# A spectral and attention kernel on one core: the inverse feature transform split into two lanes of 64 contraction rows, and a new instruction order

## The chip, the cores and the metric

One core of a Trainium2 chip runs the whole program. The metric is the device time of one execution in microseconds (us); smaller is better. Shown for the kernel before are three runs and one profiled execution.

## What is computed

The input x has 2048 rows of 640 features. Two results are mixed by a gate: a dilated local attention (32 heads of 20, each row looks at 8 rows two apart), and a spectral filter: a two-dimensional real Fourier transform of x, a multiplication by a table of complex weights, and the inverse transform.

```python
g = sigmoid((x * gate_w).sum(-1, keepdims=True))
q, k, v = split(x @ wqkv)
a = softmax(q k / sqrt(20), over 8 rows 2 apart) v @ wo
b = irfft2(rfft2(x) * (w_r + 1j * w_i))
return g * a + (1 - g) * b
```

## The kernel before, in words

The 2048 rows are handled as 16 row blocks j of 128 rows (row 16p + j of the input stands on partition p). The work falls into stages whose instructions are interleaved:

- **qkv**: x times wqkv in float32r, 8 units of 8 row blocks, 15 matmuls of 480 columns each, stored to DRAM (tile qkvd).
- **fold** and **cols**: the features are folded into their cosine and sine parts, and a 128-row transform along the rows is made; the result stands in SBUF as zg, 5 tiles t of 128 feature rows for each j.
- **attend** (16 calls, half for even j, half for odd j): VectorE (DVE) and GpSimd (POOL) make the products and sums of the attention, two row blocks at a time; results go to DRAM (tile od).
- **freq** (line 637, 16 blocks g): matmuls v and u (feature transform), sums ab on DVE, matmuls x and z (the second part of the row transform), the product with the weights, partly on POOL (tile P) and partly on DVE (in place in z), then two DVE instructions that write the tile s as P plus z and P minus z (lines 714 to 719), and five matmuls g that take 128 columns of s each as stationary operand and whose result ScalarE (ACT) copies back into zg.
- **spatial** (line 761, 16 row blocks, odd j first): the inverse feature transform and the last part of the inverse row transform. The feature part is six matmuls into two PSUM tiles, oa and ob (o1 and o2 in the code), from the stationary zg[:, t, j] and the table gt. The 640 feature rows are a cosine-even part (161), a cosine-odd part (160), a sine-even part (159) and a sine-odd part (160) one after another, so that the tiles t = 1, 2 and 3 of 128 rows straddle two parts. A straddling tile makes a 322-column matmul or two of 161. ACT copies oa and ob to the tile os, four matmuls of 161 columns make ha and hb, and DVE, ACT and POOL finish the even blocks. Banks 0, 1 and 2 of PSUM serve oa and ob in turn.
- **project_even, project_odd** (lines 843 and 857): the attention result of one row block is loaded (tile ot), transposed on TensorE (PE) into oT, multiplied by wo (30 matmuls of 320 columns in float32r, woa and wob), and added to the spectral part. An odd block can only be projected when all of its attention has been stored, and the odd blocks come last.

Matmuls of float32 operands (u, v, x, z, g, oa, ob, ha, hb) stand in the trace as two records each, one after the other: two passes, each with its own weight load (LDWEIGHTS, on the row PEld). float32r matmuls are one record.

The order in which all of this is issued is not the order of the code. Every instruction is recorded with its engine (class Plan, line 164), and ORDER (line 204), a compressed table of numbers found beforehand, says in which order they are issued. Each engine then runs its own instructions in that order. Nearly all rows of the trace carry the line of the recording helper (L385), so they are told apart by tile names.

Of the kernel before, what the change touches and what calls it, by code (L numbers as in the profile page):

```python
# [31 lines left out]
def dft_tables():  # L32
# [98 lines left out]
    gt = np.zeros((640, 644))
    gt[0:161, 0:161] = np.cos(tau * np.outer(ke, d) / D) * ck(ke)
    gt[161:321, 161:322] = np.cos(tau * np.outer(ko, d) / D) * ck(ko) * (d < 160)
    gt[321:480, 322:483] = -np.sin(tau * np.outer(kb, d) / D) * ck(kb) * ((d > 0) & (d < 160))
    gt[480:640, 483:644] = -np.sin(tau * np.outer(ko, d) / D) * ck(ko) * (d > 0)
    gt = np.concatenate(
        [gt[0:128, 0:161], gt[128:256, 0:322], gt[256:384, 161:483], gt[384:512, 322:644], gt[512:640, 483:644]], 1
    )
# [70 lines left out]
HQ(%xOkCb5Ti|9M&74oX@)~%FC+g&Um>cIj7Th&a$THElCM_Qxh94S8@_R$YuH^AlZ29A62|gtX_GwKt861v*&%|Lj%A~%)Ju4ard*J9-%@(h(=zcz=9{hy8`{2ylZ=~+70?!1ipBf(&
zwb}8-f;L(FVHcuzwYP7?2%s*U{nv&ECs$KBfw^t@z;C&Xf&zSgn_WXO0Ra-A{p=`KSTo&WCxLcHX{frWWSucqtk!hm#2nHJeX5P<a5rX;@Kti_Yl8ko7HnBP?BD0BCR!|nSp+9pO(On  # L210
7C*Q$o$wOs&SmSBdiC|DHG?D8$uS*E_ccd=5LY{i^BiXwbd{r0)D57<l%^E2DaY|53+8~ZxRJddAoRNdJYPz%5Lvh5W}S={Qu`$OJ}cwneg)RxR)(xpZMXtIs%DRMvJ7u?%%!@^1B8h@
(qlVz@tLYv`rnaOHo>WRfe{k*SBQiEnDF!z+o6MsFAJ=(MehAC+OQk;gfj{$D4Y9E8C&GfcpM}t1W|C%hJ#;L!7aan3ZqicP~xB7_Qnrj(tTe<@R?W&V{($jS4EF-5t#TOP0?OuT|3Qa
eIT(hT>jCQrecqER6AALUaUC?)=4v!RW)w9%$6TmkX}rmdZ1<A!<Ce0_LGFT-55A$ndz>!p$dHdxh1>o=3<(6z*KuxX86ZbhMDSB?~D@~6mK>u#>!XP<ORCokbE-Ovd^FevYd6|yTLNh
6LqbJKy?z;o)=#fxd)}q(t!E7s4(3|QOszQKMHHgt&?pyfYSMq-!@LPp=HMQOrhAsZ-JWy-C3Mc^Z`{5!$bngKocKj*>1lOfpe>gL<4DAk0)0!w_E-I8Ix5zA0pAPHAB79wZiA}lY^=h
Std;TST@mvK(Izv+y2xl{ZkLjAJfK%G&=WMvx-dxg6DMA424jO9cS?4TWJptst&`UzGq$ZfJ_rYlV4K31$NLXrgHytE*H`DST?S8Z+_yEBRpdjK2A~uXM4Nj32C4N!P4z2;Hqn$;QEkU
x#r;cod7g-0_+HHSjTx0G?wMOQFZ}koI>bLqzm3R1#oY}9`o)-A1NE;d6CRy2FU=-R;2owOP)Xp5@L{{lo`pBpk%V|R6g=MDVwD`bNH=OjT}S9%<^i$H2}^WSgi-blEMMxNCWOt@KVe#
HqSpv<!^C>%lNmv7RSF7$EOxNC{yKe#`U(Lx+?J!T>!ZP9DRYha-KfY6f?D)z+1)BTY#H0H8P_on~L7A?2-f-TVGlJ$NYiPg`Ivs?eZmoz*1s%9Xd;!3V#C-+$0Brl2%!N#H_A1i{L@S
P#-7P*l5}1Q+W5C%(=qlbU3pZ%otQHBXliSa7Eq92vyz1<`-h2wlnrTN(?T$K{1wyGNT3yESJ?d;(Zw=a_uas{jBg++Q~Nj2jh-_=z=SgoGX(xs<sgT2K8=TN&l`u^j-}yWbYSO(5cEw
hVcGl#lx!tpndKnI3W6}4nYMD+Pk`P27A{L32W`ao5f1Lx*Nb1X()n(JDUZ2O2az;7O<uub@cq%>A*E(_tL!Qq_R=1wNX@G<vau7PJDCp_$;h81hHJ;PIGy_$BYC9!FRj&Q%d@dloNT&
V}(@XS$iJK7_UBeT9exaHe0ZCd>(H!PSGFR8O~kQ=y2V-@rw&$Jg2mnKHs;xrCurTIvRujMxI%zzSsUAbNQyk@KBwL05WxN*Sm)5I2Xq^XZjzH)Ihl#)t51ss6A^!b?3)adQa(X1?V`Q  # L220
wEf(@vgv8sXd>1A(Inx$aDsF9o|pp|HZf+o&w(aEY-(nPPdJX2mvN>(E_fL#$UQPvI|Oa9cnbzr-e$^;-WQD_g83Pq)JF@6puq4=iw_oAzI4h0IpY+hbO=V@zz#KK7T>Y)df*No_7zw#
J`ZNS1m5yd>sTzrvwN&$9|njAQz>w>cl%q7wQZn?8p!=9m>5`9rRfIf_1}m*K9QWX2p$bk-U|1B1Z(^)NFjGTUi*=`v=?z{hl`I|qiO|ofbK~N2V}%VS*t!h=6?gk(z$O~7sEFHmYj%6
MNgL}676SI+-J!42{U}iie@2JyD7wX?tWyweu6+;9xiJSQlECBlw3cU6JNL9Qbq$0tUe_bx^QVlnRQ^tl#ei^!;Uy@((9<|ywE43$z4IgNR)3HBAWp^wA5G)i`pF3l<h}x3OgiJc*rTp
yDIhR4d;b1#P9;B=Fn!{JagvZWQ8Dna+>C8?PWN5+e!O%eKQFD7&UwCI9EJuzf24eM=px5vm)*=iSJQOsoOrV0(&B;X_MREg42C+90%XRnO_)k_RRKzcw`jk&FlJtxyJ@dT+yf~v((s8
-2h}>WX&Km>`JDrIZsB~HyMCyj)w7Emh<Bxtc+@vJ<-~GPXyd<K2@BwUFJSEEbOSLf-}5Tj30C4oH>gKhj@`yM0lgO1I|~8Uz5d)n(Ap~u7*R$VC*4V^uL@BrFYVSXJ!#;GPx$-`iB^*
2MiYfr5xOz@(Hn_ZO=uraJXL7TjCH2Oo22&4b<5GbESU)fMy@w<%JD=kBRvs^7YntD5lPeG0~#A(Y7f~=u1vSN3y;*%B)if3ZHyCNgsIjl_GRnl%27NSP+9t2PA;2H4bS5GyaV=>j*#x
*M~~EY1!7%?esLp+*GX}o-QD6C&^J6=;H8X|6(A(`yZi}Z}faaS0?Gjqv@lj&ep&tv$=yAF_CROwlnc;Gg~`p{^9llwa}e7zb`&fYr`LIz+M4&!D;pBW0~8c-9pQAVK~5|Lst>X_XHJf
BbHYtz@n{+NemE;D#YqvNyi@TUL%=x!c}A)W#~0YXI_9y%G_JmIy7up9F-wz0Ko(;nI?_m?Kd3a(}245c2v@Jf1OP32?$)b@4&S%LtI4Xl7SDnL8i5%lEDj)>G1TqOFDWr8uzjy&O3Nm
d$+wYoEer$Aq-KST1DqGF`N6nbu3i9J1y!73cVHXcW7RCc*0zmf=AnkP~}&rJ5)<G5jD!ivtsQGa!*YrUZ<x(O%YP2uxAQgki#<4cU6)m;~U+_$c%HUxDD2C>6*du+*nLhT21G%FSMTx
F9o90(I?=4__Uh>X7zl2S;|3%g?xk&&ZNy<yz%i{Sl87#;Hq(*dX#-S;0K7k`-=_DNmtn_cWizA<)OfVpjTP3DV~JDA&$35ndX-;RJ~3efGwiJ5Ht%!mBpiuzqzwAm%V<N$YT+%N<y?-  # L230
L$<-n`T;@{9ha=_DU5Caogirb*l5ll(=hVGvPaUVHGn@TTk@(O%Cg>+!F&Z>^a}MWs*HoAIXZ*IGmD&KQ1$s5UlW<f%b`0L6Zo}XxY*ejMiL6wZB3VWksk25LDcc$*m+|kO*MiA5qM!R
E4&I$iUB%e=t-&vI#oE3omS`8qhKNa{&xtjquCoj@gt~4hPP`#R?lah{_Fr2NG)2)6j`)6xWw-bn!#53kreFmg|f%8{Hi9hP;wz{AL5rvcI#V0DymT1c(Kucy<*0`8=s--Bri8zDH~#v
%-FB#M0Qq%ICg_IFP2C48|n56Sm9Um9k2fiPvpqah%)KEUW1~=uV*6=QB*z{Al8lvW9Q;ye=6Tp=v>L79H5IQ5X|z~#8hpnJr+Ga_QrkC4`Rhv7#WXovCK>ybSs8B6l~NOoIP)O5Fr!S
+}fcYgLx<p#v>wbK=gW?vhdCXZVtgKhsHNHj%~Qolp5+lQ(hjj51#p5_1_2~j|^=(cHJD!9j9&qpZdcxvk%!cXv8;;W{9m%oyJFbB38c|mac656_T8#{}Kg@00
# [732 lines left out]
```

## Time and profile before

| | |
|---|---|
| three runs | 453.57, 454.58, 453.53 us; median 453.57 |
| profiled execution, span | 454.1 us, 0.1% above the median |
| PE busy | 441.2 us, 97% (weight loads PEld 391.8 us) |
| DVE, POOL, ACT busy | 409.8 us, 363.9 us, 211.9 us |
| instructions | 7249, of them 2440 matmul records |
| DMA | 110.75 MB in 73956 packets |

A matmul's record lasts from its start to its modelled end, and records of neighbouring matmuls overlap; how long one really holds PE is the distance from its start to the next one's start. Idle time of PE is what the view of waits lists.

### The profile page before, as it was taken

Reading aid. Unit: us, or ns where it says so; the run is one execution under the profiler, and the core shown is the slowest. Engines: PE = TensorE matmul, PEld = TensorE weight load, DVE = VectorE, ACT = ScalarE, POOL = GpSimd, SP = SyncE. Lnnn points to the kernel's source line nnn. Section 1 sums busy time; section 2 is a strip of 40 time slices with the busy share of each in tenths; the row PEclk is TensorE's granted clock in tenths of the full one; section 3 lists DMA queues with packets and bytes.
Section 4 is the critical chain, followed back from the end, with each engine's and each line's share of the span. In section 5 each row is a group of like instructions: output and inputs, shape, how many; then the busy total and the mean of one; then the engine's idle time right before and its main releaser. Section 6 shows DMA issues by size and latency. Waiting matters only on the chain. (4 is left out here: it accounts for less than half of the span.)

```text
span 454.1 us, 7249 instructions
## 1 busy us (share of the span) xinstructions
PE 441.2 (97%) x2440; PEld 391.8 (86%) x2440; DVE 409.8 (90%) x519; ACT 211.9 (47%) x561; POOL 363.9 (80%) x316
## 2 busy tenths in 40 slices
PE   9999999999999999999998989999989999999996
PEld 6888888888889888899886769998877899999996
DVE  4899999899999999999978989999999997899484
ACT  4723165625226463255356666667554655342110
POOL 1158895899899898988977898976899998889810
PEclk9999999999999999999998999999999999999999
DMA  8998999887968979679979778989883331365932
GB/s 312 401 383 268 340 330 377 305 264 237 272 183 272 340 217 316 181 216 320 303 220 294 240 230 250 297 245 320 258 257 105 85 97 54 118 207 134 296 123 87
DMA packets 73956, 110.75 MB, mean 244 GB/s; under 512 B 21296, under 2 KB 50992, under 8 KB 73920
## 3 DMA queue, kind: packets, MB, share of 16 engines
q1 hardware_dynamic: 40192, 69.32, 46.8%
q10 hardware_dynamic: 32816, 36.97, 26.1%
q0 software_dynamic: 912, 4.00, 2.4%
q8 instruction: 19, 0.31, 0.3%
q14 instruction: 17, 0.14, 0.1%
HBM read 72.51 MB, written 32.84 MB: 232 GB/s over the span
## 5 line engine op out<-in xcount | busy, mean ns | idle before, releaser
L385 PE MATMUL qkv<-w,xo 128*128 128x480 f32 (+1 forms) x480 | 110.6, 385 | 0.0
L385 PE MATMUL qkv<-w,xe 128*128 128x480 f32 (+1 forms) x474 | 104.3, 382 | 0.0
L385 PEld LDWEIGHTS qkv<-w,xe 128*128 128x128 f32 x474 | 89.3, 189 | 15.2 <-ACT xe L385 0.9
L385 PEld LDWEIGHTS qkv<-w,xo 128*128 128x128 f32 x480 | 89.7, 189 | 13.8 <-ACT zg L385 0.2
L385 ACT COPY ev<-qkv 128x480 f32<-128x480 f32 x64 | 34.9, 558 | 48.3 <-PE qkv L385 35.9
L385 PE MATMUL woa<-wo,oT 128*128 128x320 f32 x240 | 47.2, 318 | 0.4 <-ACT oT L385 0.4
L385 PE MATMUL wob<-wo,oT 128*128 128x320 f32 x240 | 46.9, 315 | 0.2 <-ACT ya L385 0.2
L385 POOL TENSOR_TENSOR P<-P,wp 128x963 f32<-128x963 f32 (+1 forms) x16 | 35.4, 2212 | 6.6 <-DMA P<-X 4.0
L385 PEld LDWEIGHTS woa<-wo,oT 128*128 128x128 f32 x240 | 37.7, 188 | 1.1 <-ACT oT L385 0.6
L385 PEld LDWEIGHTS wob<-wo,oT 128*128 128x128 f32 x240 | 37.8, 188 | 0.6 <-ACT ya L385 0.4
L385 POOL TENSOR_TENSOR fx<-fx 128x160 f32<-128x160 f32 (+1 forms) x16 | 12.8, 818 | 24.2 <-DMA fc<-in_t_fc 17.1
L385 POOL TENSOR_TENSOR w<-raw,w 128x480 fp32r<-128x480 f32 (+1 forms) x20 | 24.8, 1262 | 5.3 <-ACT w L385 5.3
L385 ACT CAST oT<-oTp 128x384 fp32r<-128x384 f32 (+1 forms) x32 | 13.4, 427 | 30.9 <-PE oTp L385 17.3
L385 PEld LDWEIGHTS g<-mm,s 128*128 128x128 f32 x150 | 21.0, 190 | 7.1 <-ACT zg L385 5.0
L385 PE MATMUL g<-mm,s 128*128 128x128 f32 x150 | 23.5, 280 | 3.1 <-ACT zg L385 3.0
L385 DVE TENSOR_TENSOR oT<-oTp,oT 128x384 fp32r<-128x384 f32 (+1 forms) x32 | 15.2, 485 | 11.0 <-ACT oT L385 10.7
L385 PE MATMUL oa<-gt,zg 128*128 128x161 f32 (+1 forms) x96 | 24.0, 344 | 0.0
L385 PE MATMUL ob<-gt,zg 128*128 128x161 f32 (+1 forms) x96 | 22.0, 344 | 0.0
L385 PE MATMUL u<-bt,zc 128*128 128x240 f32 (+2 forms) x96 | 21.1, 335 | 0.7 <-DVE ab L385 0.7
L385 PE MATMUL v<-bt,zc 128*128 128x240 f32 (+2 forms) x96 | 21.5, 335 | 0.2
L385 DVE TENSOR_TENSOR fx<-fx 128x642 f32<-128x642 f32 (+2 forms) x24 | 19.2, 798 | 0.7
L385 PEld LDWEIGHTS u<-bt,zc 128*128 128x128 f32 x96 | 16.9, 199 | 2.9 <-PE g L385 0.9
(304 smaller groups left out, 1107.6 us busy)
## 6 DMA issues: line engine op xcount, KB each, us to landing
qkvd<-ev ACTq DMA_DIRECT2D x32, 480.0 KB, 4.8
wp<-in_ws SPq DMA_DIRECT2D x16, 642.0 KB, 5.9
raw<-in_wqkv SPq DMA_DIRECT2D x25, 240.0 KB, 5.9
fx<-in_x SPq DMA_DIRECT2D x8, 641.0 KB, 7.9
ot<-od SPq DMA_DIRECT2D x16, 320.0 KB, 3.9
P<-X ACTq DMA_DIRECT2D x30, 160.5 KB, 4.6
fd<-fx POOLq DMA_DIRECT2D x6, 640.0 KB, 5.6
f<-fd SPq DMA_DIRECT2D x6, 640.0 KB, 6.1
```

The costliest lines, as they stand in the source:

```text
L385: p.dve.memset(w, 0.0)
```

## The change

The feature rows are laid out anew. Lane 0 (partitions 0 to 63 of each tile t) holds 160 cosine rows and then 160 sine rows of the even frequencies, lane 1 (partitions 64 to 127) the same of the odd ones; 320 rows are exactly five strips of 64. The middle strip (t = 2) is half cosine and half sine and needs 322 columns, the other four need 161. The table `gt` becomes 128 rows of 966 columns. In `spatial` each row block now makes ten matmuls with 64 contraction rows each, five with partitions 0 to 63 into oa and five with partitions 64 to 127 into ob.

In `freq` the tile s has to be written in that layout: four DVE instructions of 256, 64, 64 and 256 elements take the place of two of 321 and 319, and one ACT instruction writes a single column. Block g = 0 has a few more. The copies of oa and ob into os become contiguous, os rotates over five buffers (before, three), and the whole of ORDER is new.

```diff
+STRIPS = (2, 0, 322), (0, 0, 161), (1, 0, 161), (3, 161, 161), (4, 161, 161)
...
 ORDER = """
-T>t<81poj4|NsC0{{R31`zHT%QmDPk&^9H>y=H*?`Lk%9Gnl%)B_CdQV7rLsIrdLM6sJFoVB8Rk|2U=URH5DLwHy3}>N|I2375U5sNENOZ_r>p;QjNS0Qt^d&3_BFn1BL!{U(U9<aW#`
...
+{Wp48S^xk5{}S0j0stWa8~^|S5YJf5;2m=ecU=Gg0s6R6M52`fc4RAY6qg`NyHIB4o@A#NU6@5pcjA0+(rn3g<Hq*N?);S;<qAiG*|7vsBv}=d&%uk^>u_xVVkn+f*DZ$G;1pjN+A)sRJO)fP3tQBb
...
-        self.osr, self.hor, self.hyr, self.yer = n("raw", 3), n("x", 4), ring("x4", "x5"), ring("x6")
+        self.osr, self.hor, self.hyr, self.yer = ring("raw0", "raw1", "raw2", "ev0", "ev1"), n("x", 4), ring("x4", "x5"), ring("x6")
...
-        V.tensor_add(s[:, 0:321], P[:, 0], z)
-        V.tensor_sub(s[:, d0 : d0 + 319], P[:, 0, 2:], z[:, 2:])
+        V.tensor_add(plus, strips(P[:, 0], 0), strips(z, 0))
...
+            V.tensor_sub(mixed[:, :, 32:64], parity(P[:, 0], 0, 32), parity(z, 0, 32))
+        V.tensor_add(mixed[:, :, 0:32], parity(P[:, 0], 128, 32), parity(z, 128, 32))
+        V.tensor_sub(minus, strips(P[:, 0], 32), strips(z, 32))
+        A.activation(out=s[:, 288:289], in_=z[:, 0:1], func=AF.Identity, bias=P[:, 0, 0:1])
...
-        mm(o1[:, 0:322], 1, gt[:, 161:483], True, False)
-        mm(o1[:, 0:161], 0, gt[:, 0:161], False, False)
-        mm(o1[:, 161:322], 2, gt[:, 483:644], False, True)
-        mm(o2[:, 0:322], 3, gt[:, 805:1127], True, False)
-        mm(o2[:, 0:161], 2, gt[:, 644:805], False, False)
-        mm(o2[:, 161:322], 4, gt[:, 1127:1288], False, True)
+        c = 0
+        for t, a, n in STRIPS:
+            for o, k in ((o1, slice(0, 64)), (o2, slice(64, 128))):
+                T.matmul(
+                    o[:, a : a + n], zg[k, t, j], gt[k, c : c + n], start=(t == 2), stop=(t == 4), skip_group_check=True
+                )
+            c += n
```

How the order changes is shown at two places. The first is PE at the start of the spatial stage. oa1 and ob1 are the two PSUM tiles of row block 1, oa3 and ob3 those of block 3, ha1 and hb1 what follows from os1; one row is one matmul of the program, "x2" two of them. Before:

```order
L385 MATMUL g15_3_815<-mm13_771,s15_813 128x128 x2
L385 MATMUL oa1_872<-gt_327,zg_211 128x322
L385 MATMUL oa1_872<-gt_327,zg_211 128x161 x2
L385 MATMUL oa3_878<-gt_327,zg_211 128x322
L385 MATMUL ob1_873<-gt_327,zg_211 128x322
L385 MATMUL ob1_873<-gt_327,zg_211 128x161 x2
L385 MATMUL oa3_878<-gt_327,zg_211 128x161 x2
L385 MATMUL ha1_875<-os1_874,fct_71 128x161
L385 MATMUL ob3_879<-gt_327,zg_211 128x322
L385 MATMUL ha1_875<-os1_874,fct_71 128x161
L385 MATMUL hb1_876<-os1_874,fct_71 128x161
L385 MATMUL oa5_883<-gt_327,zg_211 128x322
```

and after the change:

```order
L384 MATMUL g15_3_815<-mm13_771,s15_813 128x128 x2
L384 MATMUL oa1_872<-gt_327,zg_211 128x322
L384 MATMUL ob1_873<-gt_327,zg_211 128x322
L384 MATMUL oa1_872<-gt_327,zg_211 128x161 x2
L384 MATMUL ob1_873<-gt_327,zg_211 128x161
L384 MATMUL oa3_878<-gt_327,zg_211 128x322
L384 MATMUL ob1_873<-gt_327,zg_211 128x161
L384 MATMUL oa1_872<-gt_327,zg_211 128x161
L384 MATMUL ob1_873<-gt_327,zg_211 128x161
L384 MATMUL oa1_872<-gt_327,zg_211 128x161
L384 MATMUL ob1_873<-gt_327,zg_211 128x161
L384 MATMUL oa3_878<-gt_327,zg_211 128x161 x3
```

The matmuls of oa and ob, which stood between those of ha, hb, wo and the transposes, now stand in nine runs over all row blocks, alternating between the lanes for the most part; the first seven runs hold 18 to 30 of the 160 matmuls each, the last two 4 and 6.

The second place is DVE in the frequency stage at block 1. ab0 are the sums of the block three steps later, pr and o tiles belong to the attention. Before:

```order
L385 RECIPROCAL g_73<-g_73 128x16
L385 TENSOR_TENSOR z1_609<-z1_609,P1_607 128x321
L385 TENSOR_TENSOR s1_617<-P1_607,z1_609 128x321
L385 TENSOR_TENSOR s1_617<-P1_607,z1_609 128x319
L385 TENSOR_TENSOR ab0_641<-u0_640,vs0_639 128x321 x2
```

and after the change:

```order
L384 TENSOR_TENSOR z1_609<-z1_609,P1_607 128x321
L384 TENSOR_TENSOR ab0_641<-u0_640,vs0_639 128x321
L384 TENSOR_TENSOR s1_617<-P1_607,z1_609 128x2x32
L384 TENSOR_TENSOR s1_617<-P1_607,z1_609 128x2x2x64 x2
L384 TENSOR_TENSOR s1_617<-P1_607,z1_609 128x2x32
L384 TENSOR_TENSOR ab0_641<-u0_640,vs0_639 128x321
```

The two instructions that write s1 have become four, and the first of the two that write ab0 has moved ahead of them.

## Rows read from the trace of the kernel before

**Rows 1.** Page, part 1: busy time, share of the span, instructions of each engine

```profile
span 454.1 us, 7249 instructions
...
PE 441.2 (97%) x2440; PEld 391.8 (86%) x2440; DVE 409.8 (90%) x519; ACT 211.9 (47%) x561; POOL 363.9 (80%) x316
```

**Rows 2.** What PE waited for, whole span: engine, releaser, us, times, longest

```profile
PE g L385 <- ACT zg L385: 3.0, 5, 1.0
PE x L385 <- DVE ab L385: 2.0, 1, 2.0
PE z L385 <- DVE t L385: 1.2, 1, 1.2
PE warmed L385 <- DVE warm L385: 1.1, 1, 1.1
```

**Rows 3.** Busy us by stretch: length, PE, PEld, DVE, ACT, POOL, clock, DMA, GB/s

```profile
220.00:260.00 40.00, 37.12 (x180) 31.27 (x179) 35.48 (x44) 22.60 (x69) 32.19 (x29) 0.96 0.86 265
260.00:346.00 86.00, 81.87 (x522) 73.66 (x521) 80.64 (x128) 53.15 (x147) 75.73 (x56) 1.00 0.84 258
346.00:409.00 63.00, 62.43 (x391) 56.90 (x390) 56.68 (x77) 30.36 (x79) 56.11 (x46) 1.00 0.34 105
```

**Rows 4.** The chain that ended last, from 346 us on: start, us, what

```profile
371.64 0.55 PE ha L385 x4
...
448.29 1.92 PE wob L385 x13
450.23 0.55 DVE y L385
```

**Rows 5.** PE in order of time, 364 to 368 us: start, us, what

```profile
365.80 0.70 PE L385 MATMUL oa<-gt,zg 128*128 128x322 f32 x2
366.34 0.44 PE L385 MATMUL ha<-os,fct 128*128 128x161 f32 x2
366.61 0.44 PE L385 MATMUL oa<-gt,zg 128*128 128x161 f32 x2
```

**Rows 6.** Group on PE by shape: count, busy, mean ns of one record

```profile
L385 PE MATMUL oa<-gt,zg 128*128 128x161 f32 x64 | 13.5, 299 | 0.0
```

**Rows 7.** Weight loads (PEld) and PE around 362 and 411 us, in order of time

```profile
361.85 0.33 PEld L385 LDWEIGHTS ha<-os,fct 128*128 128x128 f32 x2
...
361.71 0.44 PE L385 MATMUL oa<-gt,zg 128*128 128x161 f32 x2
...
410.91 0.19 PEld L385 LDWEIGHTS woa<-wo,oT 128*128 128x128 f32 x1 [0.59 <-ACT oT L385]
410.91 0.42 PE L385 MATMUL woa<-wo,oT 128*128 128x320 f32 x1 [0.35 <-ACT oT L385]
411.01 0.19 PEld L385 LDWEIGHTS wob<-wo,oT 128*128 128x128 f32 x1
...
411.17 0.31 PE L385 MATMUL wob<-wo,oT 128*128 128x320 f32 x1
```

**Rows 8.** Groups on DVE and ACT by shape: count, busy, mean ns

```profile
L385 DVE TENSOR_TENSOR s<-P,z 128x321 f32<-128x321 f32 x15 | 7.3, 486 | 0.9 <-POOL P L385 0.2
L385 DVE TENSOR_TENSOR s<-P,z 128x319 f32<-128x319 f32 x15 | 7.2, 480 | 0.0
...
L385 DVE TENSOR_TENSOR ye<-ho 128x160 f32<-128x160 f32 x8 | 2.3, 317 | 0.0
...
L385 ACT COPY z<-qkv 128x1 f32<-128x1 f32 x16 | 2.5, 162 | 1.7 <-ACT ev L385 1.7
```

**Rows 9.** SP's queue, stores and loads of the attention result, in order of time

```profile
421.66 0.37 SPq L385 DMA_DIRECT2D od<-o4b  x1
...
427.00 0.32 SPq L385 DMA_DIRECT2D ot<-od  x1
...
431.51 0.33 SPq L385 DMA_DIRECT2D ot<-od  x1
```

More of the change, by code (lines that the diff above doesn't have):

```diff
@@ L129, in ck @@
         return (np.where((k == 0) | (k == 320), 1.0, 2.0) / (S * D))[:, None]
[L131 to L138, printed above, removed]
+    lanes = np.zeros((2, 320, 322))
+    for lane, k, fits in ((0, PERM[1:161], (d > 0) & (d < 160)), (1, ko, d > 0)):
+        c = np.cos(tau * np.outer(k, d) / D) * ck(k) * ((d < 160) | (lane == 0))
+        s = -np.sin(tau * np.outer(k, d) / D) * ck(k) * fits
+        lanes[lane, 0:160, 0:161], lanes[lane, 160:320, 161:322] = c, s
+    lanes[0, 160] = np.repeat([1.0, 0.0], 161) / (S * D)
+    lanes = lanes.reshape(2, 5, 64, 322)
+    gt = np.concatenate([lanes[:, t, :, a : a + n].reshape(128, n) for t, a, n in STRIPS], 1)
     f = np.float32
@@ L209 @@
[L209 to L216, printed above, removed]
@@ L354, in work @@
         S.dma_start(self.sign, ins["t_sign"])
-        self.bt, self.gt = self.one("bt", 1288, tag="e0"), self.one("gt", 1288, tag="e1")
-        S.dma_start(self.bt[:, 0:1122], ins["t_bt"])
+        self.bt, self.gt = self.one("bt", 1122, tag="e0"), self.one("gt", 966, tag="e1")
+        S.dma_start(self.bt, ins["t_bt"])
         S.dma_start(self.gt, ins["t_gt"])
@@ L714, in freq, with parity, strips @@
         s = self.s12r.next(f"s{g}", 768)
-        d0 = 321
-        if g == 0:
-            d0 = 449
-            G.memset(s[:, 384:449], 0.0)
-        V.tensor_add(s[:, 0:321], P[:, 0], z)
-        V.tensor_sub(s[:, d0 : d0 + 319], P[:, 0, 2:], z[:, 2:])
+        def parity(a, k, n):
+            return a[:, 1:321].rearrange("p (b k) -> p b k", b=2)[:, :, k : k + n]
+        def strips(a, k):
+            return parity(a, k, 128).rearrange("p b (t r) -> p b t r", t=2)
+        plus, mixed, minus = (s[:, 128 * t : 128 * t + 128 * n] for t, n in ((0, 2), (2, 1), (3, 2)))
+        plus, minus = (q.rearrange("p (t b r) -> p b t r", t=2, b=2) for q in (plus, minus))
+        mixed = mixed.rearrange("p (b r) -> p b r", b=2)
+        V.tensor_add(plus, strips(P[:, 0], 0), strips(z, 0))
+        if g == 0:
+            other = s[:, 640:768].rearrange("p (b r) -> p b r", b=2)
+            G.memset(s[:, 256:384], 0.0)
+            G.memset(s[:, 640:768], 0.0)
+            for b in range(2):
+                V.tensor_sub(other[:, b, 33 - b : 64], parity(P[:, 0], 1 - b, 31 + b)[:, b], parity(z, 1 - b, 31 + b)[:, b])
+        else:
+            V.tensor_sub(mixed[:, :, 32:64], parity(P[:, 0], 0, 32), parity(z, 0, 32))
+        V.tensor_add(mixed[:, :, 0:32], parity(P[:, 0], 128, 32), parity(z, 128, 32))
+        V.tensor_sub(minus, strips(P[:, 0], 32), strips(z, 32))
+        A.activation(out=s[:, 288:289], in_=z[:, 0:1], func=AF.Identity, bias=P[:, 0, 0:1])
         yield
-        last = s[:, 640:768] if g == 0 else s[:, 512:640]
-        chunks = [[(s[:, 0:128], 0)], [(s[:, 128:256], 0)], [(s[:, 256:384], 0)], [(s[:, 384:512], 1)], [(last, 1)]]
-        if g == 0:
-            chunks[2:4] = [[(s[:, 384:512], 1), (s[:, 256:321], 0)], [(s[:, 512:640], 1)]]
         for t0, n in ((0, 3), (3, 2)):
```

63 lines of the change are left out of this document (33 added, 30 removed).

## The prediction

> **What bounds the kernel now.** I read the page first: PE is busy 441.2 us of a span of 454.1 us [rows 1], and the weight loads overlap the matmuls, so PE comes first. The waits of PE say how much of the span it stands still for others: the four longest releasers make 7.3 us in all, nearly all of it in the frequency stage [rows 2]. By stretch, PE loses 2.9 of 40 us and 4.1 of 86 us there, but only 0.6 of 63 us between 346 and 409 us, where the spatial stage lies, and the granted clock is 1.00 from 260 us on [rows 3]. The chain that ended last runs over PE almost alone through the spatial stage and the projections to the last wob, with a DVE step at 450.23 us behind it [rows 4]. So in the spatial stage a microsecond that PE no longer needs should come off the end, as long as the projections that follow have their data. DVE is almost as full: 56.7 of 63 us there and 80.6 of 86 us before [rows 3].
>
> **What is removed on PE.** In order of time, an oa of 322 columns starts at 365.80 us and the next matmul at 366.34: 0.54 us. One of 161 columns holds PE from 366.34 to 366.61: 0.27 us [rows 5]. I count in units of 0.27 us. A row block now costs two matmuls of 322 and four of 161 columns, 8 units; 16 blocks are 128 units, 34.6 us. After the change each lane has one matmul of 322 and four of 161, 6 units. If lanes 0 and 1 work at the same time, that is 16 times 6 = 96 units, 25.9 us: **-8.6 us**. No row of this trace shows two matmuls of 64 rows side by side, so this bound is the assumption on which the forecast stands; the far end is two lanes one after the other, 192 units, 17.3 us more than now.
>
> **What stays empty in the lanes.** The new order does not pair the lanes perfectly. oa3 has three matmuls of 161 columns one behind the other while lane 1 has nothing, because ob3 takes the bank that oa1 leaves (three banks for oa and ob). Counting along the nine runs with each matmul starting when its lane is free and the one ahead of it has started, I get 107 units, 11 more than 96: **+3.0 us**. The bounds: if a lane never waits for the other one, the longer lane of each run makes 102 units (+1.6 us). If the two passes of a float32 matmul must both have started before the next matmul may start, the lanes work one pass apart, and the same count over passes gives 115 units (+5.1 us). I take the middle one, since inside a steady alternation a stagger of one pass costs nothing and is paid mainly at the ends of a run.
>
> **What the borders cost.** Nine runs have 18 borders between matmuls of 64 rows and of 128. The trace has only one kind, so I bound a border. Below: nothing. Above: the record of a 161-column pass lasts 0.299 us [rows 6] of which 0.135 us is its turn (half of 0.27), so 0.16 us of it run on beside the next one; if that tail must run out and the next weights load only then, a border costs 0.16 + 0.11 = 0.27 us. The 0.11 us is a load that nothing hides: after the wait at 410.91 us the first woa lasts 0.42 us where the next wob, of the same form, lasts 0.31, and the next load starts 0.10 us after the first [rows 7]. That restart is the nearest row, so I take 0.11 us for each: 18 x 0.11 = **+2.0 us**, between 0 and 4.9.
>
> A rule bears on weight loads: in "TensorE: Matmul & The Clock Gate" (Part 3, The mechanism) the Trainium skill says that a load overlaps a running matmul only when the two use different row groups. The trace disagrees: a load of 128 rows for ha starts at 361.85 us while the oa of 128 rows that started at 361.71 still runs [rows 7], and a pass keeps its turn of 0.135 us. By the rule each of the 192 passes of oa and ob would have paid its 0.11 us of load, and the change would give some 20 us more (-24 instead of -3.1); I put nothing for it into the sum.
>
> **What is added in the frequency stage.** The two s instructions on DVE take 0.486 and 0.480 us; one of 160 elements takes 0.317 us [rows 8], so 161 more elements cost 0.169 us: 1.05 ns each over a fixed 0.15 us. 256 elements then cost 0.42 us and 64 cost 0.22 us: 2 x 0.42 + 2 x 0.22 = 1.27 against 0.97 us, 0.30 us a block, 4.8 us over 16 blocks. The single column on ACT is nearest to the copy of one column, 0.162 us [rows 8], 2.6 us in all. On the path this would count only where PE waits for s: the waits of PE name ab, t and the copies to zg, not s [rows 2]. What is queued behind s on DVE is the next block's ab, which PE does wait for, though the new order puts one of the two ab sums ahead of s. I take **+0.5 us**, between 0 (all of it in DVE's idle 9.9 us of that stage: 40 - 35.5 and 86 - 80.6 [rows 3]) and 4.8. The smaller gt, the contiguous copies into os and the five os buffers remove no wait that a row shows: 0.
>
> **The rest of the order.** The frequency stage keeps its sequence on PE, so I take 0. It cannot save much more than half of the 7.3 us, and may lose as much: -4 to +4.
>
> **The sum**: -8.6 + 3.0 + 2.0 + 0.5 = -3.1 us. The profiled execution (454.1 us span) is 0.5 us above the median of 453.57 us; from the median I forecast **450.5 us**. A measurement of this kernel can tell about 0.3% from no change, 1.4 us: under 452.2 is faster, over 454.9 slower.
>
> **The rivals.**
> - *Weight loads in line (slower).* If the loads of both lanes use one path, a turn of 161 columns needs 2 x 0.11 us of loads against 0.135 us of matmul. A pair of 161 columns (two turns) then takes 0.44 instead of 0.27 us, 0.17 more; 64 such pairs make 10.9 us, of which up to 3.0 lie in the empty units counted above: -3.1 + 7.9 = +4.8, **458.4 us**. It decides from the point where the second load adds over 0.02 us to a turn. For it: a load that nothing hides takes 0.10 us from start to start [rows 7]. Against it: nothing but that the lanes lie on different partitions. No overlap of matmuls at all, that the change does not do what it says, belongs here: more than 465 us.
> - *Drained borders (no change).* Each of the 18 borders at its upper bound: -8.6 + 3.0 + 4.9 + 0.5 = -0.2, **453.4 us**. For it: the tail of 0.16 us behind each pass. With the staggered count too it would be 455.5. The Trainium skill has this as a rule ("TensorEngine Tiling (Array Packing)", Key Properties: a change of tiling mode drains the engine); no row here shows a border.
> - *The attention sets the end (no change).* The last o4b is stored at 421.66 us and the last ot loads are issued at 427.00 and 431.51 us [rows 9]. With DVE 4.8 us later and PE 3.1 us earlier, the last two odd blocks would wait: the end stays near **453.5 us**. Against it: DVE has 6.3 us idle between 346 and 409 us [rows 3], some of it waiting for PE.
> - *Free lanes and fewer holes (more).* Lanes at 102 units, half of the waits of the frequency stage gone, -3.1 - 1.4 - 3 = -7.5: **446 us**.
>
> **How the numbers follow.** Forecast (about 449 to 452) 0.42, free lanes 0.12, drained borders 0.16, attention 0.08, loads in line or no overlap 0.22. Faster: the forecast and the free lanes, and 0.01 of the others: 0.55. No change: drained borders and attention, less the 0.02 of them that end over 454.9: 0.22. Slower: 0.23. The range of 8 in 10 reaches from 446 (the free-lane case) to 458.5 (loads in line); it leaves out the case of no overlap and the ends of the bounds. The likeliest case's own range is 448 to 452.2.
>
> **What would show it.** Right: in the spatial stage matmuls of oa and ob start within the same 0.27 us of each other, a row block's ten matmuls take about 1.8 us in a run, and the span from the first oa to the last transposes shrinks by 3 to 4 us, with the tail of projections as long as before. Borders: the distance from the last 64-row matmul of a run to the first 128-row one, against 0.135 us. Wrong by loads: loads of oa and ob 0.1 us apart and matmul starts to match. Wrong by attention: waits of woa for oT at the end. DVE's s groups should read 0.42 and 0.22 us. A time over 455 or under 446 us would mean that the lanes do not behave as counted.

## The result, and the profile after

| | before | after |
|---|---|---|
| median of 8 runs each, one chip | 453.51 us (452.77 to 454.58) | 455.38 us (454.32 to 457.57) |
| ratio, 95% interval | | 1.0041 [1.0021, 1.0061] |
| again on another chip, 35 and 12 runs | 453.94 us | 455.27 us, 1.0027 [1.0009, 1.0045] |

The change is slower, by 1.3 to 1.9 us, where 3.1 us less were forecast. A ratio compares all executions of two kernels, so it is not always the quotient of the two medians shown. Three executions stand apart and are left out of the ratios below: two of six_matmuls (1131 and 1557 us; its only trace is of the second) and one of dc_early (469 us).

The kernel after was profiled in an execution of 455.52 us. Its span is 453.6 us: outside the span lie 1.9 us, and 1.7 to 2.1 us in the other executions of the two kernels for which both are on record. The prediction set a span against a median of times and left this out: by these numbers the profiled execution of before took some 455.9 us, an estimate, 2.3 us over its median, and its granted clock was 0.96 between 220 and 260 us [rows 3], where after had 1.00. So the two traces are of executions about as long, differences in time are taken from the other runs, and part of the waits of before may belong to that execution alone.

The page of after, part 1 [rows 1]:

```profile
span 453.6 us, 7554 instructions
...
PE 441.7 (97%) x2568; PEld 388.9 (86%) x2568; DVE 410.2 (90%) x552; ACT 212.5 (47%) x577; POOL 361.6 (80%) x317
```

PE is as busy as before, though its 160 matmuls of oa and ob were to take a quarter less. The busy time by stretch, columns as in [rows 3]:

```profile
220.00:260.00 40.00, 38.95 (x200) 33.16 (x200) 39.52 (x52) 25.34 (x81) 37.87 (x31) 1.00 0.84 245
260.00:346.00 86.00, 82.30 (x517) 72.57 (x515) 80.04 (x154) 56.27 (x162) 73.63 (x57) 1.00 0.86 263
346.00:409.00 63.00, 62.19 (x515) 55.76 (x516) 57.08 (x79) 30.62 (x81) 57.27 (x47) 1.00 0.37 110
```

What PE waited for in the whole span [rows 2]:

```profile
PE z L384 <- ACT s L384: 1.9, 3, 1.1
PE g L384 <- DVE s L384: 1.1, 2, 0.6
PE warmed L384 <- DVE warm L384: 1.1, 1, 1.1
...
PE woa L384 <- DVE oT L384: 0.6, 2, 0.4
...
PE g L384 <- ACT zg L384: 0.4, 1, 0.4
```

The long waits of before for zg, ab and t (3.0, 2.0 and 1.2 us [rows 2]) are gone or short. Waits for s, of which before had none among the longest, stand at the head, the first of them for ACT's column. The sum does not show the loss: between 225 and 350 us PE's waits make 4.5 us in after and 7.1 in before. What the stage costs is found below by leaving instructions out. Now the lanes: PE in order of time in the first run of oa and ob and at its two borders, PEld at its start, and ACT's first copy of oa [rows 5, 7].

```profile
346.68 0.54 PE L384 MATMUL oa<-gt,zg 64*128 64x322 f32 x1
346.69 0.54 PE L384 MATMUL ob<-gt,zg 64*128 64x322 f32 x1
347.06 0.43 PE L384 MATMUL oa<-gt,zg 64*128 64x322 f32 x1
347.06 0.43 PE L384 MATMUL ob<-gt,zg 64*128 64x322 f32 x1
347.33 0.30 PE L384 MATMUL oa<-gt,zg 64*128 64x161 f32 x1
347.33 0.40 PE L384 MATMUL ob<-gt,zg 64*128 64x161 f32 x1
...
348.69 1.12 PE L384 MATMUL oa<-gt,zg 64*128 64x161 f32 x7
349.65 0.54 PE L384 MATMUL ob<-gt,zg 64*128 64x322 f32 x1
...
351.12 0.43 PE L384 MATMUL ob<-gt,zg 64*128 64x161 f32 x2
351.48 0.82 PE L384 MATMUL hb<-os,fct 128*128 128x161 f32 x4
...
346.68 0.18 PEld L384 LDWEIGHTS oa<-gt,zg 64*128 64x128 f32 x1
346.69 0.18 PEld L384 LDWEIGHTS ob<-gt,zg 64*128 64x128 f32 x1
...
349.17 0.43 ACT L384 COPY os<-oa 128x322 f32<-128x322 f32 x1 [2.00 <-PE oa L384]
```

The two lanes run side by side: at the head of the run the loads of oa and ob start within 0.01 us of each other, and so do their matmuls; later the lanes are up to 0.1 us apart. The first row block's ten matmuls take 2.3 us and not the forecast 1.8: they end with the second of the seven records at 348.69, and 0.54 us of the time is a matmul of block 3 in lane 0. The hole at 348.69 is seen too: seven records of oa one after the other, while lane 1 starts nothing until 349.65, just when ACT has copied block 1's oa out of the bank that lane 1 takes next (349.17 to 349.60). And so is a border: the first pass holds PE 0.38 us (346.68 to 347.06), the next of the same form 0.27; at the run's end hb starts 0.36 us after the first of the last two ob, whose two turns are 0.27.

Groups by shape: count, busy us, mean ns of one, then idle time before [rows 8].

```profile
L384 DVE TENSOR_TENSOR s<-P,z 128x256 f32<-128x256 f32 x30 | 12.2, 416 | 1.6 <-POOL P L384 0.7 <-ACT s L384 0.4
...
L384 DVE TENSOR_TENSOR s<-P,z 128x64 f32<-128x64 f32 x30 | 5.9, 215 | 0.2
...
L384 ACT ACTIVATE s<-z,P 128x1 f32<-128x1 f32 x15 | 3.9, 261 | 12.9 <-DVE s L384 12.7
```

The pieces of s last 416 and 215 ns, where 0.42 and 0.22 us were worked out; the column lasts 261 ns, and ACT stands idle 12.9 us in front of its 15 instances. One of them, on ACT, DVE and PE in turn:

```profile
311.99 0.38 ACT L384 COPY zg<-g 128x256 f32<-128x256 f32 x1
314.63 0.26 ACT L384 ACTIVATE s<-z,P 128x1 f32<-128x1 f32 x1 [2.26 <-DVE s L384]
314.79 0.20 ACT L384 COPY L5a<-low 1x16 f32<-1x16 f32 x1
314.88 0.51 ACT L384 COPY zc<-zg 128x384 f32<-128x384 f32 x1
...
313.52 1.02 DVE L384 TENSOR_TENSOR s<-P,z 128x256 f32<-128x256 f32 x4 [0.33 <-POOL P L384]
315.02 0.42 DVE L384 TENSOR_REDUCE m5a<-L5a 128x32 f32<-128x256 f32 x1 [0.48 <-ACT L5a L384]
...
314.94 0.81 PE L384 MATMUL z<-ab,mm 128*128 128x321 f32 x2 [1.13 <-ACT s L384]
```

ACT is done with zg at 312.37 us and stands in front of the column until DVE has written all of s (313.52 to 314.54). Behind the column, in ACT's order, stand a small copy, for which DVE then waits 0.48 us, and a copy to zc. PE's z waits 1.13 us, since the column is the last to read the bank that it will take. Of all waits between 225 and 350 us, the longest, and PEld's for the column:

```profile
ACT s L384 <- DVE s L384: 12.7, 12, 2.3
...
PEld z L384 <- ACT s L384: 3.5, 6, 1.4
```

### The profile page after: what moved, and what is told of

It reads as the page before. It is cut to its first block, busy times and chain, and to the rows that moved or that the text cites. A ratio compares the mean times of both kernels' runs of the same rounds, so it can differ in the third digit from the quotient of the medians.

```text
span 453.6 us, 7554 instructions
## 1 busy us (share of the span) xinstructions
PE 441.7 (97%) x2568; PEld 388.9 (86%) x2568; DVE 410.2 (90%) x552; ACT 212.5 (47%) x577; POOL 361.6 (80%) x317
## 4 chain that ended last, share of the span: by engine, by line
PE 63%; DVE 16%; POOL 6%; DMA 6%; issue 4%; ACT 3%; ACTq 1%; DVEq 0%; SPq 0%; POOLq 0%
PE qkv L384 33%; PE wob L384 6%; PE woa L384 6%; PE z L384 5%; DVE fx L384 2%; POOL P L384 2%; DVE s L384 2%; POOL fx L384 2%; POOL w L384 2%; PE ob L384 2%; PE oa L384 2%; DMA fx<-in_x 2%; DMA st<-in_w 2%; PE u L384 2%; PE v L384 2%
## 5 line engine op out<-in xcount | busy, mean ns | idle before, releaser
L384 PE MATMUL qkv<-w,xo 128*128 128x480 f32 (+1 forms) x480 | 118.2, 390 | 0.0
L384 PE MATMUL qkv<-w,xe 128*128 128x480 f32 (+1 forms) x474 | 106.8, 383 | 1.4 <-POOL w L384 0.6
L384 PE MATMUL wob<-wo,oT 128*128 128x320 f32 x240 | 49.4, 323 | 0.2 <-ACT ya L384 0.2
L384 POOL TENSOR_TENSOR fx<-fx 128x158 f32<-128x158 f32 (+1 forms) x16 | 11.9, 753 | 26.0 <-DVE fx L384 25.5
L384 PE MATMUL ob<-gt,zg 64*128 64x161 f32 (+1 forms) x160 | 31.2, 336 | 0.0
L384 PE MATMUL oa<-gt,zg 64*128 64x161 f32 (+1 forms) x160 | 30.5, 336 | 0.0
L384 PE MATMUL g<-mm,s 128*128 128x128 f32 x150 | 25.6, 280 | 1.6 <-DVE s L384 1.1
L384 PEld LDWEIGHTS ob<-gt,zg 64*128 64x128 f32 x160 | 23.8, 186 | 2.2 <-issue 0.9
L384 PEld LDWEIGHTS oa<-gt,zg 64*128 64x128 f32 x160 | 23.7, 186 | 1.9 <-issue 0.6
L384 ACT CAST w<-raw 128x480 fp32r<-128x480 f32 (+1 forms) x30 | 17.2, 592 | 9.2 <-DMA qkvd<-ev 4.8
```

The lines of the kernel that those rows point to most:

```text
L384: p.dve.memset(w, 0.0)
```

## Experiments

Theory A at first: the lanes overlap, and their gain is eaten by the holes in the runs and the borders. Rivals: lanes that hardly overlap (B), a gain that is there and is given back in the frequency stage (C, later divided into E, the column that ACT waits for, and F, the further small instructions on DVE), and a loss in the order (D). All of these kernels have the new order: where an instruction is left out, its place in the order is passed over, and where one is added or moved, it is issued together with the one before it. Ratios are to the kernel before on the same chip.

### What the lanes give

`full_rows` and `one_group`: all ten matmuls of a row block with 128 rows; both lanes on the same 64 partitions. Both compute other sums.

```diff
-            for o, k in ((o1, slice(0, 64)), (o2, slice(64, 128))):
+            for o, k in ((o1, slice(0, 128)), (o2, slice(0, 128))):   # full_rows
+            for o, k in ((o1, slice(0, 64)), (o2, slice(0, 64))):     # one_group
```

> The order and all else as after the change, but each of the ten lane matmuls of a row block takes all 128 rows (zg[:, t, j] and gt[:, ...]), so that nothing overlaps and no border between 64 and 128 rows is left; the spectral result is then not the reference's. Theory A (the gain is used up inside the spatial stage): the trace of after shows 31.0 us in the nine runs and about 0.2 us at each of 18 borders, 34.6 us; here 192 units of 0.272 us, 52.2 us, 17.6 us more, no border: 473 us. Rival B (the lanes hardly overlap): only a few us more than 455.4, under 462 us.

> As after the change, but both lanes take partitions 0 to 63, the same half of the array; the spectral result is then not the reference's. Theory A: the lanes gain only because their row groups differ; 52.2 us of matmuls one behind the other, as with full rows, and the 18 borders on top at 0.2 us: 3.6 us over full_rows, 476 to 477 us; a 128-row matmul behind a 64-row run starts about 0.2 us late, as in after. If a border costs nothing and the 0.2 us was something else, the same as full_rows within 1 us.

Measured: 472.91 us, 1.0402 [1.0364, 1.0439], and 475.56 us, 1.0467 [1.0417, 1.0517]. Without the overlap the kernel takes 17.5 us more than after, so the overlap is real and Rival B falls. (The prediction's far end, 17.3 us, was counted from before; from there it is 18.8 us.) In the second run the lanes stand in line as well, and it has the 18 borders that the first has not: 2.65 us, 0.15 us for each, where 3.6 us were expected.

`six_matmuls`: as much work as before in oa and ob, six matmuls of 128 rows, everything else as after. The sums are others.

```diff
+                if t in (1, 3):
+                    p.skip()
+                    continue
-                T.matmul(o[:, a : a + n], zg[k, t, j], gt[k, c : c + n], ...)
+                T.matmul(o[:, a : a + n], zg[:, t, j], gt[:, c : c + n], ...)
```

> The lanes alone undone: order, s and layout as after the change, but oa and ob are each made of three matmuls of 128 rows (322, 161, 161 columns), as before the change, at the places of three of the five lane matmuls; the spectral result is then not the reference's. Theory A: 34.8 us of matmuls take the place of 31.0 + 3.6 us, so the time is that of after within 1 us, 454.4 to 456.4. Rival C (the lanes do save about 3 us net, and the added instructions in the frequency stage or the order take it back): 457.5 to 459 us.

Measured: 456.35 us, 1.0043 [1.0021, 1.0064], in Theory A's range: with the s of after, the lanes are worth 0.4 us by the ratios and 1.0 us by the medians, and the intervals overlap. Most of their gain goes into holes and borders, as Theory A has it, but that would leave the kernel level with before, not 1.3 to 1.9 us behind it.

### What the frequency stage costs

`six_and_s` also writes s by two instructions and without the column in blocks 1 to 15; `lanes_old_s` does this alone and keeps the lanes. In both the rows of s stand in the old order and the zero feature of these blocks is left out.

```diff
+        if g:
+            V.tensor_add(s[:, 0:321], P[:, 0], z)
+            V.tensor_sub(s[:, 321:640], P[:, 0, 2:], z[:, 2:])
```

> The arithmetic of before in the new order: as six_matmuls, and for blocks g from 1 to 15 s is written by two DVE instructions of 321 and 319 elements, without the single column on ACT; the spectral result is then not the reference's. Difference to before: the order and block 0. Theory A with a quiet frequency stage: within 1 us of six_matmuls. Rival C, frequency stage: 2 to 3 us under six_matmuls, as PE waits 3.3 us for s in after. Rival D (the new order itself loses): still 1.5 us or more over before, 455 us or more.

> After the change with lanes, but s written by two DVE instructions and no column, for g from 1 to 15 (result wrong). Theory A (lanes net nothing): within 1 us of six_and_s, 451.5 to 453.5 us. If the lanes gain once the frequency stage no longer hides it: under 450.5 us.

> The lanes with s written by two DVE instructions and no column, a second time on another chip, since the kernel without the column alone came out at 0.9968 on one chip and 0.9996 on another, so that one run does not tell what the two further DVE instructions cost. It leaves out the new layout of s (the rows of s stand in the old order) and the column in blocks 1 to 15. If the two further DVE instructions cost 2 us or more: 451 to 452.3 us, ratio 0.992 to 0.996. Rival (they are hidden, and the first run was scatter): 453.2 to 454.2, ratio 0.998 to 1.000.

Measured: 452.53 us, 0.9962 [0.9938, 0.9986]; 451.65 us, 0.9935 [0.991, 0.9961], and a second time 452.60 us, 0.9946 [0.9917, 0.9976] (the expectation speaks of another chip, the record names chip 0 for both). So the additions cost about 4 us by the ratios (1.0034, the mean of after's two ratios, less 0.9940), 2.7 to 3.7 us by the medians of the same runs, and 3.7 us between six_matmuls and six_and_s. Of Rival C the cost holds and the gain of 3 us does not. With the additions gone the lanes are worth 0.9940 against six matmuls' 0.9962, 1 us, which these intervals do not separate from nothing.

`before_new_order` is the kernel before, its arithmetic and all, in the new order and with five buffers for os.

> The kernel before with the new order alone: its own arithmetic in every stage, all instructions at the places that the new order gives their counterparts, os over five buffers; the two instructions that write s stand where the first two of the new ones stood. Theory A (lanes net nothing, s costs about 3.8 us, the order gains): as six_and_s, 452 to 453 us, 1.5 us under before. If the order gains nothing by itself and six_and_s owed its time to something else: 454 us or more.

Measured: 454.15 us, 0.9984 [0.996, 1.0009]. By itself the order gives some 0.7 us or nothing; Theory A's 452 to 453 us are missed, and six_and_s, which does nearly the same work, lies 1.6 us lower.

The traces, one execution each, divide the time at the first matmul of oa or ob. From there to the end of the span it is 106.6 us in before, 107.8 and 107.5 us with six matmuls in the new order (six_and_s, before_new_order), 106.4 us in both traces of lanes_old_s and 106.9 us in after. So in this part the lanes take 1.1 to 1.4 us off, and the new order puts 0.9 to 1.2 us on. What the additions cost lies ahead of it: the first oa or ob starts at 342.2 and 344.9 us with six matmuls, at 344.7 and 345.8 us in lanes_old_s, and at 346.7 us in after.

`no_column` leaves out the column alone, `two_dve` keeps the column and writes s by two instructions.

```diff
+        if g:
+            p.skip()
+        else:
+            A.activation(out=s[:, 288:289], in_=z[:, 0:1], func=AF.Identity, bias=P[:, 0, 0:1])
```

> After the change without the single column that ACT writes into s, for blocks g from 1 to 15 (the constant feature of these blocks is then wrong); the four DVE instructions stay. In after, PE waits 2.2 us for this column (z and iz for ACT s) and 1.1 us for DVE s. Theory E (the column holds the bank of z, and that is the cost): 2 to 3.5 us less than after, 452 to 453.4 us. Rival F (the longer DVE work is the cost; then z waits for DVE's last s instead): at most 1 us less, 454.4 us or more.

> After the change with lanes and the ACT column, but s is written by two DVE instructions of 321 and 319 elements in place of four, for g from 1 to 15 (its layout is then not what the lanes need, so the result is wrong). Saves 0.3 us of DVE a block, 4.5 us in all. Theory E (the column): at most 1 us less than after, 454.4 us or more. Rival F (DVE's time): 2.5 to 3.8 us less, 451.5 to 453 us.

Measured: 453.14 us, 0.9968 [0.9949, 0.9987], and 454.40 us, 0.9998 [0.9979, 1.0017]. Both hit what Theory E expected, the second at the very edge. But both parts cost something, the column more, by these runs: beside lanes_old_s on the same chip (451.65 us), the two further DVE instructions make 1.5 us and the column 2.8 us.

### Is the instruction paid, or its place?

`col_on_dve`: the same sum on DVE at the column's old place in the order.

```diff
-        A.activation(out=s[:, 288:289], in_=z[:, 0:1], func=AF.Identity, bias=P[:, 0, 0:1])
+        V.tensor_add(s[:, 288:289], P[:, 0, 0:1], z[:, 0:1])
```

> The kernel after, but the single column of s is added on DVE (s[:, 288] = P plus z, one element a partition) at the same place of the order, not by ACT. Theory E (the column is dear because ACT works in order and stands in front of it until DVE has finished z and s: 12.7 us of ACT's time between 225 and 350 us, with copies that PE needs queued behind): the 3.3 us that came back without the column come back here too, less the new DVE instruction, about 0.16 us x 16 = 2.6 us of DVE time of which I count a third on the path: 453.0 to 454.0 us, ratio to the kernel before 0.997 to 1.000. Rival F (a fifth small instruction that reads z and must be done before the matmuls g costs the same wherever it stands): 455.0 to 455.8 us, ratio 1.003 to 1.006. ACT's wait for DVE's s should vanish from the trace in either case.

Measured: 461.52 us, 1.0164 [1.0144, 1.0185], outside both expectations. The trace shows why, DVE, then ACT, then PE in order of time:

```profile
285.55 1.00 DVE L384 TENSOR_TENSOR s<-P,z 128x256 f32<-128x256 f32 x4
286.48 1.48 DVE L384 TENSOR_REDUCE L5a<-pr5a 128x64 f32<-128x1280 f32 x1
287.99 1.49 DVE L384 TENSOR_TENSOR pr5a<-kt5a,qbank 128x1280 f32<-128x1280 f32 x1
289.40 1.48 DVE L384 TENSOR_REDUCE o7b<-pv7b 128x160 f32<-128x1280 f32 x1
290.79 0.14 DVE L384 TENSOR_TENSOR s<-P,z 128x1 f32<-128x1 f32 x1
296.63 0.42 DVE L384 TENSOR_REDUCE s6b<-L6b 128x32 f32<-128x256 f32 x1 [5.69 <-ACT L6b L384]
...
291.98 0.53 ACT L384 ACTIVATE X<-z,sign 128x321 f32<-128x321 f32 x1 [4.29 <-PE z L384]
...
296.17 0.42 ACT L384 ACTIVATE L6b<-L6b 128x256 f32<-128x256 f32 x1
...
290.99 0.95 PE L384 MATMUL z<-ab,mm 128*128 128x321 f32 x2 [3.86 <-DVE s L384]
```

In this block the four s were done at 286.5 us, but on DVE the column's place lies behind three instructions of 1.5 us. It ends at 290.9, and until then z's bank is held. PE's next z waits 3.86 us, ACT waits 4.29 us for it to make X, L6b stands behind X on ACT, and DVE, which made the column, waits 5.69 us for L6b. A place in a common order is another place on every engine.

`dc_early` gets rid of the column with the same result: the features are reordered so that a minus instruction writes the zero feature's slot, and ACT turns the sign of two weights per partition after the exchange has been issued (one matmul each of v and u grows from 240 to 241 columns by it). `dc_early_zfree` also writes the last step of z to SBUF, which frees z's bank sooner.

```diff
+            A.mul(wp[:, 2:4, 0:1], wp[:, 2:4, 0:1], -1.0)
...
# dc_early_zfree; s then reads P[:, 2] for z
-            V.tensor_sub(z, z, P[:, 2])
+            z = P[:, 2]
+            V.tensor_sub(z, wide["z"][:, 0:321], z)
```

> The kernel after with the same result but without the column in 15 of 16 blocks: the features are put in the order zero, even ones, 320, odd ones, and the zero feature's two weights that act on z change their sign on ACT as soon as the exchange of x and z has been issued (one ACT instruction on 2 numbers a partition), so that the minus instruction of 64 numbers writes the zero feature's sum itself. Theory E (what is dear is ACT's wait for DVE's late result, not one more small ACT instruction): as without the column, 452.6 to 453.6 us, ratio 0.996 to 0.999. Rival (a small ACT instruction of some 0.2 us a block costs by itself, by delaying what is behind it on ACT): 454.5 to 455.5 us, ratio 1.001 to 1.004.

> The kernel of the early sign change, and besides the last step of z (the difference with P) writes to SBUF, into P's third part, and no longer in place into z's PSUM bank, so that the bank is free three to four DVE instructions sooner (about 1 us) in 15 of 16 blocks. Theory Z (PE's waits of z for s, 0.9 us in all without the column and 1.9 us in the kernel after, come from the bank that s still reads): these waits vanish, 451.9 to 452.8 us, ratio 0.995 to 0.997, 0.5 to 1 us under the run with the early sign change alone. Rival (the bank's wait only takes the place of waits for s or ab that come right behind it): no difference from the run with the early sign change, within 0.3 us.

Measured: 461.36 us, 1.016 [1.0119, 1.02], and 489.73 us, 1.078 [1.0758, 1.0802]. Both theories missed both. In the first, ACT now stands in front of the sign until weights have landed; ACT's wait for it:

```profile
ACT wp L395 <- DMA wp<-in_ws: 12.3, 7, 4.9
```

ACT stands 12.3 us in front of that small instruction, seven times, the longest 4.9 us: the nearest cause that the trace shows for the new loss, not tested by a run. The second is another matter, told at the end.

`col_next` puts the column on DVE directly behind the last s. `packed` needs no column: lane 0 has its 161 sums and then 31 differences, lane 1 has 32 differences between its sums, so that the differences of the middle strip are 63 neighbours; gt's rows are moved to match.

```diff
# col_next, issued together with the s instruction before it
+        V.tensor_add(s[:, 288:289], P[:, 0, 0:1], z[:, 0:1])
# packed
+            V.tensor_add(view(s, 256, 95)[:, :, 0:33], view(Pf, 128, 160)[:, :, 0:33], view(zf, 128, 160)[:, :, 0:33])
+            V.tensor_sub(s[:, 289:352], Pf[:, 130:193], zf[:, 130:193])
```

> The kernel after, with the column of s added on DVE directly behind the last of the four s instructions, not at the column's old place in the order. In the run with the column on DVE at its old place one column stood behind three long attention instructions (1.48 us each, s done at 286.5 us, column at 290.8 us) and z's bank with it. Theory E (what is dear is how long the column comes after s, on whichever engine): 0.16 us more of DVE a block and nothing in line, 453.0 to 454.2 us, ratio 0.997 to 1.0005, and no wait of PE for s over 1.5 us. Rival F (a fifth small instruction on z and s costs wherever it stands, since DVE is full): 454.8 to 456, ratio 1.002 to 1.005.

> The kernel after with the same result but no column at all: the rows of the two lanes are put in another order (lane 0 has its 161 sums first and then 31 of its differences, lane 1 has 32 differences in the middle of its sums), so that four DVE instructions of 256, 66, 63 and 256 numbers write all of s in 15 of 16 blocks and nothing is left for ACT. gt's rows are moved to match; matmuls, widths and the order are as they were. Theory E: as in the run without the column, 452.5 to 453.7 us, ratio 0.995 to 0.999, so under both kernels. Rival (the gain of that run came from the work that it left out, not from the queue): 454.5 to 455.5.

Measured: 454.25 us, 1.0004 [0.9984, 1.0024], and 454.88 us, 1.0013 [0.999, 1.0036]. The first has the ratio that Theory E gave it, and a time at the end of its range (454.2 us); the second falls in its rival's range, so here Theory E missed. Since single executions scatter by 1 us and more, these kernels were then run side by side on one chip:

> The changed kernel itself, on the same chip and in the same rounds as the three kernels without the column, with it on DVE and with the packed s, because the differences of 1 to 3 us between them were so far taken across chips, while executions of one kernel scatter by 1 us and more. Theory E (the waiting column costs 2 to 3 us): 455 to 456 us, ratio 1.002 to 1.006, at least 1.5 us over the next three. Rival (those differences were scatter between chips): within 0.7 us of them.

> Without the column in blocks 1 to 15 (it leaves out the zero feature of these blocks). Theory E: 452.5 to 454 us, ratio 0.996 to 0.999. Rival: within 0.7 us of the changed kernel.

> The packed s, four DVE instructions and no column with the same result. It issues the same instructions on every engine in the same places as the kernel without the column, but for one ACT instruction in block 0. Theory E: as the kernel without the column, 452.5 to 454 us. Rival (leaving out the column saves something that packing does not save): 454.5 to 455.5, over 1 us more than without the column.

> The column on DVE directly behind s. Theory E: 453 to 454.5 us, ratio 0.997 to 1.001, 1 us or more under the changed kernel. Rival F (the instruction costs wherever it stands): as the changed kernel within 0.7 us.

| | us | ratio |
|---|---|---|
| after | 455.27 | 1.0027 [1.0009, 1.0045] |
| without the column | 453.79 | 0.9996 [0.9972, 1.002] |
| packed | 454.00 | 0.9996 [0.9964, 1.0029] |
| column on DVE behind s | 453.68 | 1.0000 [0.9986, 1.0014] |

The last three agree within 0.3 us and lie 1.3 to 1.6 us under after, where Theory E wanted 1.5 us or more. Taken one by one their intervals overlap that of after; what carries the reading is that three kernels made in three ways agree. The instruction itself costs nothing that these runs can tell (col_next issues it 16 times on a nearly full DVE); its place on ACT is paid. The waits of ACT in the first trace of col_next (of its fastest execution, 451.51 us) between 225 and 350 us begin with a wait that after has too, and the one for s is gone; PE's longest waits there are for s still, 0.7 us in two:

```profile
ACT zg L395 <- PE g L395: 8.0, 12, 1.6
...
PE g L395 <- DVE s L395: 0.7, 2, 0.5
...
PE z L395 <- DVE s L395: 0.2, 1, 0.2
```

No version with the full result beats the kernel before by more than a measurement can tell; col_next and packed come level with it.

## Why the prediction was wrong

Term by term, in us against before; the measured column takes means of the ratios above, times 454, where it does not name the traces:

| term | predicted | measured |
|---|---|---|
| lanes: overlap, holes, borders | -8.6 + 3.0 + 2.0 = -3.6 | -0.2 by the records of after; -1.1 to -1.4 by the length of the stage in the traces; -0.4 (six_matmuls) and -1.5 (lanes_old_s against the mean of six_and_s and before_new_order) by the runs |
| additions in the frequency stage | +0.5 (0 to 4.8) | +4 (2.7 to 4.8, by the pair of runs taken) |
| rest of the order | 0 (-4 to +4) | -1.2 (-0.7 and -1.7) |
| sum | -3.1 | +1.3 to +1.9 |

Two terms failed, the larger one first.

- **The failed step is "I take +0.5 us" for the added work of the frequency stage.** It measured about 4 us, near its upper bound. The sizes were right (416 and 215 ns for 0.42 and 0.22 us). What was wrong is the ground for hiding them: the waits of PE named ab, t and zg and not s [rows 2], so s was taken to have room. The long wait in front of PE said who came last in that order, not who would be next, and PEld, whose waits the prediction did not show, already waited 0.5 us for s in before. DVE's idle time in that stage did shrink, from 9.9 us to 6.4 (40 - 39.5 and 86 - 80.0), but room on DVE somewhere in the stage is not room between z and the matmuls that need s. For the column I priced a duration, 0.162 us from [rows 8], and not the wait in front of it: 12.7 us of ACT. The side-by-side runs put 1.3 to 1.6 us on the column; what is left, some 2.5 us, is then on the two further DVE instructions (lanes_old_s at a mean of 0.9940 against 0.9996, the mean of the six runs without the column or with it on DVE behind s). The runs of one chip (lanes_old_s, no_column, two_dve) divide it the other way, 2.8 and 1.5 us, so the division is open.
- **The lanes' term was right in its mechanism and too good in its sizes: -3.6 us were forecast, and -0.2 to -1.5 came.** The overlap of -8.6 holds. The nine runs span 31.0 us in the trace where half of all lane work is 26.2, so holes cost 4.8 instead of 3.0, close to the count by passes (5.1) that I had set aside. By the records 1.8 us of them stand before the 322-column matmul that opens a tile, where, as at 349.65, a lane waits for one of three banks, and 1.4 us at the ends of the runs, where one lane is done before the other. The 18 borders cost 0.19 us each by the records, 3.4 us, and 0.15 us by one_group, instead of 2.0. The spatial matmuls of oa and ob thus take 34.4 us, where the prediction counted 34.6 for before. The sign that it asked for failed too: from the first oa to the last transpose it is 96.0 us in before and 97.0 us in after, not 3 to 4 us less.
- **The order** was taken as 0 and gives about 1.2 us (the mean of before_new_order and six_and_s, 0.9973), hardly more than these two runs differ by. Its ground, that PE keeps its sequence in the frequency stage, does not hold: before starts with v and then u (229.32 and 229.73 us), after with u and then v (231.39 and 233.21 us). The missing waits for zg, ab and t point the same way, though the one trace of before is of an execution 2.3 us over its median. (Of the 7.3 us of waits that the prediction put nearly all into the frequency stage, the 1.1 us for warm lie at the kernel's start.) The order hides part of the loss.
- **The rivals.** Loads in line falls: the loads of both lanes start together. Drained borders came nearest in mechanism, at 0.19 of the 0.27 us supposed; alone it would have been no loss. With the staggered count the prediction gave it 455.5 us, and 455.4 came: that is luck, since this sum puts +1.4 us on the lanes and 0.5 us on the additions. Attention does not set the end: PE's waits of woa for oT are 0.6 us in all. No rival had the column in ACT's queue: the slower side of the forecast rested on another mechanism.
- **The range** (446 to 458.5) held the time by luck: its upper bound is that of a rival that did not happen.

How the three parts add is known to about 1 us. Longer runs and a fourth bank for oa and ob were not tried. That the additions cost more than the lanes and the order give is shown; how the cost divides between the column and the DVE instructions is not.

## What to carry to other kernels

Price a small instruction that is added to an engine working in order by the wait in front of it and by the buffer that it is the last to read, not by its duration: look up when its inputs are ready and what is queued behind it. When the longest waits are removed from a full pipeline, the next producer in the chain becomes the last one, so "nobody waits for it" in the old trace is no room for more work there. Lanes of half the rows do overlap, but each change between 64 and 128 rows and each hand-over of a bank comes off a gain of 0.27 us a pair, and in this kernel they took nearly all of it.
